# Order and cut of the first loads in a decode step: a 512 KB block of keys first, wq in four transfers, head 0's values in two

## The chip, the core and the metric

The kernel runs on one core of one Trainium2 chip. The core has five engines with a program each: TensorE (PE in the profile, its weight loads PEld), VectorE (DVE), ScalarE (ACT), GpSimd (POOL) and SyncE (SP), which here does little but issue transfers. Transfers between HBM and the on-chip memory SBUF run on 16 DMA engines that all issuers share. SBUF has 128 partitions; a transfer moves one row, a run of bytes, into each. The metric is the device time of one execution in microseconds (us); lower is better.

## What is computed

One token goes through an attention block with a key and value cache and through a gated feed-forward block:

```
h  = x + Attention(layernorm(x), k_cache, v_cache, wq, wo)
     q = layernorm(x) @ wq                      # 512 -> 32 heads of 128
     scores = q . k * 128**-0.5                 # 8 key heads, 65536 positions, 4 query heads for each
     o = softmax(scores) . v
     Attention = o @ wo                         # 4096 -> 512
h2 = h + (sigmoid(hn @ w_gate) * (hn @ w_up)) @ w_down,  hn = layernorm(h)
```

All inputs are bf16. The caches are 8 heads of 65,536 positions of 128 values, 16.78 MB for one head's keys and as much for its values; wq and wo are 4.19 MB each, the three feed-forward matrices 1.84 MB each. Together 282.33 MB are read once, for one token.

## The kernel before

**Staging.** A *chunk* is 2,048 positions of one head: 512 KB, on each partition 16 positions or 4 KB. A head's keys are 32 chunks, its values too. They pass through `ring`, a buffer of 36 chunks; `ktw` holds first wq (4 MB), then, as 8 chunk slots, the transposed keys, and last wo. A head is loaded in halves of 16 chunks (8.39 MB): K.0, V.0 of the head before, K.1, V.1 of the head before. Head 0's keys differ: they come in four transfers of 8 chunks into free space of the ring and wait for nothing.

**Loading.** All large loads are issued by SyncE, one after the other, in the order in which they are written (lines 341 to 374). A load that overwrites space waits for its last reader: an `F` mark of VectorE (line 528, a tiny memset to `scr` that stands behind the last transpose of a region) or a `PV` mark of TensorE. SyncE stops at such a wait, and all issues behind it stop too. Head 1's first keys wait for F0.0, which stands behind 16 transposes of head 0; head 0's first values wait for F0.1, behind 32. The first load of SyncE (wq) and the first of ScalarE (x) are moved ahead of the barrier at the program's start.

**Which position lies where.** In a transfer partition p takes a contiguous run of the cache, so a transfer of 16 chunks gives partition p the positions 256p to 256p+255 of its half. Softmax does not care for the order of positions as long as keys and values of one head use the same.

**Compute of a head.** VectorE transposes each chunk in 32x32 blocks from `ring` to `ktw` (line 525), TensorE multiplies it with the query weights (line 443, four passes for each chunk, in groups of four chunks), VectorE takes the maximum, ScalarE the exponentials (line 571), VectorE transposes them, and TensorE multiplies them with the values (line 443 again, `ring` and `PT_sb`). ScalarE copies a head's query weights into `ktw` (`head_weights`, line 494) behind the exponentials of the head before. Chunks are taken in the order 4 to 15, 0 to 3, 16 to 31.

**Start.** x is loaded into `xs` and spread by a small matmul (line 423) and two VectorE operations to `x_col`, where partition p holds the elements 4p to 4p+3. Layernorm makes `xz` of it (line 432). TensorE then projects q (`project_q`, line 466): 32 matmuls over wq, whose partition p holds the rows 4p to 4p+3. q goes through ScalarE and a VectorE transpose (lines 480, 483) into `qz`, and only then is `ktw` free for the first transposed keys: head 0's first transpose waits for q.

Of the kernel before, what the change touches and what calls it, by code (L numbers as in the profile page):

```python
# [9 lines left out]
AF = mybir.ActivationFunctionType  # L10
ALU = mybir.AluOpType
# [4 lines left out]
NQ = 32  # L16
DH = 128
# [3 lines left out]
TC = 16  # L21
# [3 lines left out]
NKT = 8  # L25
# [10 lines left out]
class Prog:  # L36
# [14 lines left out]
    def op(self, eng, fn, deps=(), name=None, to=None, times=1):  # L51
        assert name is None or name not in self.where, name
        self.ops[eng].append(dict(fn=fn, deps=[d for d in deps if d], name=name, dma=None, to=to, times=times, part=self.part.get(eng)))
        if name:
            self.where[name] = (eng, len(self.ops[eng]) - 1)

    def dma(self, eng, fn, sem, deps=(), name=None):
        self.op(eng, fn, deps, name)
        rec = self.dma_sems.setdefault(sem, dict(sem=None, count=0))
        rec["count"] += 16  # L60
        self.ops[eng][-1]["dma"] = (sem, rec["count"])
# [162 lines left out]
def bass_sequential_preLN__gqa_block_cached__glu_gated_glu__decode_kernel(  # L224
# [10 lines left out]
    CH = TC * DH  # L235
    PIECES = ((0, 16), (16, 32))
# [10 lines left out]
    with ExitStack() as es:  # L247
# [3 lines left out]
        gsel = sb("gsel", [128, 128], fp32)  # L251
        hz = sb("hz", [128, 128], fp32)
        identf = sb("identf", [128, 128], fp32)
        onesf = sb("onesf", [128, 128], fp32)
        lsel = sb("lsel", [128, 128], fp32)
        iota_i = sb("iota_i", [128, 128], i32)
        ident = sb("ident", [128, 128], bf16)
# [6 lines left out]
        ring = sb("ring", [128, RING], bf16)  # L264
        ktw = sb("ktw", [128, NKT * CH + WH], bf16)
# [3 lines left out]
        qz = sb("qz", [128, 8 * 64], bf16)  # L269
# [2 lines left out]
        one_f = sb("one_f", [1, 1], fp32)  # L272
        zcol = sb("zcol", [128, 1], bf16)
        zf = sb("zf", [128, 1], fp32)
        XR = 16
        xs = sb("xs", [XR, D // XR], bf16)
        xpick = sb("xpick", [XR, 128], bf16)
        xmask = sb("xmask", [128, 128 // XR], fp32)
        xm = sb("xm", [128, D // XR], fp32)
        x_col = sb("x_col", [128, 4], fp32)  # L280
        xz = sb("xz", [128, 4 * 16], bf16)
        qh = sb("qh", [32, 512], bf16)
        qt = sb("qt", [32, 512], bf16)
        hT = [sb(f"hT{i}", [128, 4], fp32) for i in range(2)]
        sq = sb("sq", [128, 4], fp32)
        st = [sb(f"st{i}", [128, 2], fp32) for i in range(2)]
        mo = [sb(f"mo{i}", [128, 4], fp32) for i in range(2)]
        rstd = [sb(f"rstd{i}", [128, 1], fp32) for i in range(2)]
# [26 lines left out]
        def ps(bank, c0, c1, p0=0, p1=128):  # L315
            return PS[p0:p1, bank * 512 + c0: bank * 512 + c1]
# [5 lines left out]
        op, dma = P.op, P.dma  # L322


        dma("act", lambda e: e.dma_start(xs[:, :], A_x[0].rearrange("o (s j) -> (o s) j", s=XR)), "x", name="x")
        W_SPLIT = {"wg": [(0, 4)], "wu": [(0, 4)]}
# [6 lines left out]
        def load(k, h, q, deps, sem, name, cols=None):  # L333
            j0, j1 = PIECES[q]
            a, z = cols or (j0, j1)
            cache = A_k_cache if k == "K" else A_v_cache
            rows = cache[0, h, j0 * TC * 128:j1 * TC * 128, :].rearrange("(p t) d -> p (t d)", p=128)
            at = (first_chunk(k, h, q) - j0) * CH
            dma("sp", lambda e: e.dma_start(ring[:, at + a * CH:at + z * CH], rows[:, (a - j0) * CH:(z - j0) * CH]), sem, deps, name)

        dma("sp", lambda e: e.dma_start(ktw[:, 0:NKT * CH].rearrange("p (k n) -> p k n", k=4),
                                        A_wq.rearrange("(p k) n -> p k n", p=128)), "r0", (), "wq")
        for q in range(2):
            for i in range(2):
                j0 = 16 * q + 8 * i
                load("K", 0, q, (), f"r{2 * q + i + 1}", f"K0.{q}{'ab'[i]}", (j0, j0 + 8))
        for h in range(1, HKV):
            load("K", h, 0, ["F0.0" if h == 1 else f"F{h - 1}.1"], "ka", f"K{h}.0")
            load("V", h - 1, 0, ["F0.1" if h == 1 else f"PV{h - 2}.3"], "va", f"V{h - 1}.0")
            load("K", h, 1, [f"F{h}.0"], "kb", f"K{h}.1")  # L350
            load("V", h - 1, 1, [f"PV{h - 1}.1"], "vb", f"V{h - 1}.1")
        h = HKV - 1
# [11 lines left out]
        for k, w in (("wg", B_w_gate), ("wu", B_w_up)):  # L364
            src = w.rearrange("(p k) n -> p (k n)", p=128)
            for i, (k0, k1) in enumerate(W_SPLIT[k]):
                at = W_AT[k]
                dma("sp", lambda e, at=at, w=src, a=k0 * FF, z=k1 * FF: e.dma_start(ring[:, at + a:at + z], w[:, a:z]),  # L368
                    f"{k}{i}", [f"PV{HKV - 1}.1"] if k == "wg" else (), f"{k}.{i}")
        src = B_w_down.rearrange("(p r) n -> p r n", p=128)  # L370
        for i, (r0, r1) in enumerate(WD_SPLIT):
            at = AT["wd"] * CH
# [33 lines left out]
        def ln_rstd(i, bank, c0, factor):  # L406

            op("dve", lambda e: e.tensor_scalar(mo[i][:, 0:2], ps(bank, c0, c0 + 2), 1.0 / D, None, op0=ALU.mult),
               [f"tot.{i}"], f"mo.{i}")
            op("dve", lambda e: e.tensor_tensor(mo[i][:, 2:3], mo[i][:, 0:1], mo[i][:, 0:1], ALU.mult), [f"mo.{i}"], f"m2.{i}")  # L410
            op("dve", lambda e: e.tensor_tensor(mo[i][:, 3:4], mo[i][:, 1:2], mo[i][:, 2:3], ALU.subtract), [f"m2.{i}"], f"var.{i}")
            op("dve", lambda e: e.tensor_scalar(ve[i][:, :], mo[i][:, 3:4], eps, factor, op0=ALU.add, op1=ALU.mult),  # L412
               [f"var.{i}"], f"ve.{i}")
            op("pool", lambda e: e.tensor_tensor(rstd[i][:, :], ve[i][:, :], nhalf[:, :], ALU.pow), [f"ve.{i}", "nhalf"],  # L414
               f"rstd.{i}")


        n = 128 // XR
        op("dve", lambda e: e.tensor_copy(xpick[:, :].rearrange("s (u i) -> s u i", i=n),
# [8 lines left out]
        op("dve", lambda e: None, ["zf"])  # L428
        ln_stats(0, (x_col[:, :], bass.AP(tensor=zf, offset=0, ap=[[1, 128], [0, 4]])), "xcol", 0, 0)
        ln_rstd(0, 0, 0, 1.0)  # L430
        xz_dst = bass.AP(tensor=xz, offset=31, ap=[[4 * 16, 128], [-8, 4]])
        op("dve", lambda e: e.tensor_scalar(xz_dst, hT[0][:, :], mo[0][:, 0:1], rstd[0][:, 0:1], op0=ALU.subtract,
                                            op1=ALU.mult), ["rstd.0", "xz0"], "xz")
        def addr_of(t, elements=0):
            return nc.lookup_mloc(t).addr + 2 * elements

# [39 lines left out]

        op("act", lambda e: e.activation(ps(1, 0, 512, 0, 8), bass.AP(tensor=zcol, offset=0, ap=[[1, 8], [0, 512]]), AF.Copy), ["zcol"], "zq")
        op("act", lambda e: e.activation(ps(5, 0, 512), bass.AP(tensor=zcol, offset=0, ap=[[1, 128], [0, 512]]), AF.Copy), (), "zy")
        op("pe", project_q, ["zq", "zy", "xz", "wq", "identf", "lsel", "onef", "sel", "gsel", "row", "PTz", "qz0"], "q")
        op("act", lambda e: e.activation(  # L480
            bass.AP(tensor=qh, offset=0, ap=[[512, 8], [64, 8], [32, 2], [1, 32]]), psap(1, 0, [[64, 8], [1, 2], [2, 32]], 0, 8), AF.Copy),
           ["q", "qh0"], "qh")
# [7 lines left out]
        def head_weights(h):  # L490

            dst = bass.AP(tensor=ktw, offset=W0 + NC - 1, ap=[[KTW_ROW, 128], [WJ, 4], [NC, 16]])
            src = bass.AP(tensor=qz, offset=64 * h, ap=[[512, 128], [16, 4], [1, 16]])
            op("act", lambda e: e.activation(dst, src, AF.Copy), ["qz", "Wz"] if h == 0 else (), f"W{h}", to="W")

        def clear_out(h):

# [10 lines left out]
        def dve_block(b):  # L508
            h, r = b // NR, b % NR
            for c in range(NC):  # L510
                n, s = b * NC + c, r * NC + c
                j = ORDER[s]
                q = sum(j >= z for _, z in PIECES)
                at = (first_chunk("K", h, q) + j - PIECES[q][0]) * CH
                src = ring[:, at:at + CH].bitcast(fp32)
                dst = ktw[:, (n % NKT) * CH:(n % NKT + 1) * CH].bitcast(fp32)
                if h == 0:
                    deps = [f"K0.{q}{'ab'[j % 16 // 8]}"] if s in (0, 4, 16, 24) else []
                    if s == 0:
                        deps.append("q")  # L520
                else:
                    deps = [f"K{h}.{q}"] if s in (0, 16) else []
                if r:
                    deps.append(f"S{b - 1}.{c}")
                op("dve", lambda e, d=dst, sr=src: e.transpose(d, sr), deps, f"T{b}.{c}", to="T")  # L525
                mark = ({15: 0, 31: 1} if h == 0 else {11: 0, 27: 1}).get(s)
                if mark is not None:
                    op("dve", lambda e, m=4 * h + mark: e.memset(scr[:, m:m + 1], 0.0), (), f"F{h}.{mark}")  # L528
            if b % NR == NR - 1:
                for k in range(NR):  # L530
                    u = b - NR + 1 + k
                    op("dve", lambda e, u=u: e.tensor_reduce(M_sb[:, u % 4:u % 4 + 1], ps(u % NS, 0, 512), AX.X, ALU.max),  # L532
                       [f"S{b}.{NC - NR + k}"], f"mx{u}", to="D")
                op("dve", lambda e: e.memset(scr[:, 32 + b // NR:33 + b // NR], 0.0), (), f"G{b // NR}")
# [255 lines left out]
        for i in range(HKV + 1):  # L790
            loop, last = 0 < i < HKV, i == HKV
            for r in range(NR):
# [26 lines left out]
                if not last and r == 3:  # L819
# [9 lines left out]
                                                   op0=ALU.mult, op1=ALU.add), ["tot.1"], "hc")  # L829
# [6 lines left out]
        for i, (nm, bank) in enumerate((("wg", GB), ("wu", UB))):  # L836
            at = W_AT[nm]
            for kt in range(4):
                for c in range(4):
# [3 lines left out]
                        rhs=ring[:, at + kt * FF + c * FG: at + kt * FF + (c + 1) * FG],  # L843
                        start=(kt == 0), stop=(kt == 3), tile_position=(0, 32 * c)),
# [66 lines left out]
```

## Time and profile before

| | |
|---|---|
| median of 3 runs (lowest, highest) | 656.7 us (656.45, 657.0) |
| the profiled execution, its own time | 656.39 us |
| span of the profile | 655.1 us |
| TensorE busy (matmuls) | 403.4 us, 62% |
| VectorE busy | 350.4 us, 53% |
| ScalarE busy | 43.1 us, 7% |
| mean granted clock of TensorE | 0.779 |

The span runs from the first to the last instruction of the profiled execution; the rest of its own time lies before and after. Busy shares are means over the whole span and do not say which engine sets the end: VectorE and TensorE work on a head's chunks side by side, and each waits for the other and for transfers in turn. The page also gives the packets and bytes of each DMA queue, and a chain of waits that is followed back from the last instruction to whatever released it, step by step. A transfer in that chain is counted from its issue to its landing, also while it only stands behind others.

### The profile page before, as it was taken

The page shows a single profiled execution, that of the slowest core. Times are in us where ns is not written, and L with a number is a line of the kernel's source. Part 1 is how long each engine was busy: PE and PEld are TensorE (multiplying, and loading weights), DVE is VectorE, ACT ScalarE, POOL GpSimd, SP SyncE. Part 2 cuts the span into 40 slices and gives each one's busy share as a digit, 9 for nine tenths or more (in the row PEclk, how much of TensorE's full clock was granted, in tenths as well). Part 3 has the DMA queues.
Part 4 walks back from the last instruction along what each step waited for, and adds up shares of the span by engine and source line. Part 5 has one row for each costly group of instructions (what it writes and reads, how often), then busy time and mean ns, then how long its engine had stood idle before and what let it go on. Part 6 is the DMA issues. An engine that isn't in the chain of part 4 may idle for free.

```text
span 655.1 us, 6215 instructions
## 1 busy us (share of the span) xinstructions
PE 403.4 (62%) x2317; PEld 65.8 (10%) x1549; DVE 350.4 (53%) x428; ACT 43.1 (7%) x114; POOL 3.7 (1%) x19
## 2 busy tenths in 40 slices
PE   2698672938648293774828467392855839285466
PEld 0100010110101000010100101010010101001122
DVE  3399853819366290935719184481917548093202
ACT  1100200020000200002000200002000020001001
POOL 1000000000000000000000000000000000000000
PEclk9899795966959588685968769596885959779665
DMA  9999999998999999999999999999999999999998
GB/s 386 446 422 474 420 412 448 448 448 388 444 448 448 436 396 448 448 448 400 432 448 448 436 396 448 448 448 408 424 448 448 444 392 444 448 448 424 422 407 363
DMA packets 6372, 282.33 MB, mean 431 GB/s; under 512 B 738, under 2 KB 868, under 8 KB 1252
## 3 DMA queue, kind: packets, MB, share of 16 engines
q1 hardware_dynamic: 6340, 282.33, 99.7%
q10 hardware_dynamic: 32, 0.00, 0.0%
HBM read 282.33 MB, written 0.00 MB: 431 GB/s over the span
## 4 chain that ended last, share of the span: by engine, by line
DMA 63%; DVE 32%; PE 3%; issue 1%; SPq 0%; ACT 0%; PEldq 0%
DMA ring<-in_A_k_cache_dram 53%; DVE ktw L525 32%; DMA ring<-in_B_w_down_dram 5%; DMA ring<-in_A_v_cache_dram 4%; PE PS L443 3%; DMA ktw<-in_A_wq_dram 2%; SPq L373 0%; SPq L368 0%; ACT qh L480 0%; PE PS L860 0%; PE PS L475 0%; DVE y_sb L878 0%; PEldq L171 0%; DVE scr L528 0%; DVE qt L483 0%
## 5 line engine op out<-in xcount | busy, mean ns | idle before, releaser
L525 DVE STREAM_TRANSPOSE ktw<-ring 128x1024 f32<-128x1024 f32 x256 | 291.6, 1207 | 160.3 <-DMA ring<-in_A_k_cache_dram 160.2
L443 PE MATMUL PS<-ktw 128*128 128x512 bf16 x1024 | 276.7, 421 | 156.6 <-DVE ktw L525 156.5
L443 PE MATMUL PS<-ring,PT_sb 128*32 x1024 | 87.7, 432 | 55.4 <-issue 46.5
L443 PEld LDWEIGHTS PS<-ktw 128*128 x256 | 26.3, 103 | 395.8 <-issue 233.5
L612 ACT ACTIVATE po_sb<-PS,rl 128x512 bf16<-128x512 f32 x8 | 5.5, 687 | 523.6 <-PE PS L443 523.6
L443 PEld LDWEIGHTS PS<-ring,PT_sb 128*32 x1024 | 20.6, 116 | 119.5 <-issue 118.2
L560 DVE TENSOR_REDUCE gmj<-PS 1x4 f32<-1x128 f32 x8 | 2.2, 279 | 54.3 <-PE PS L558 54.3
L532 DVE TENSOR_REDUCE M_sb<-PS 128x1 f32<-128x512 f32 x32 | 19.9, 683 | 19.3 <-PE PS L443 19.3
L571 ACT ACTIVATE P_sb<-PS,negmax 128x512 bf16<-128x512 f32 x32 | 21.6, 686 | 0.3
L581 DVE STREAM_TRANSPOSE PT_sb<-P_sb 128x512 bf16<-128x512 bf16 x32 | 19.9, 677 | 1.5 <-ACT P_sb L571 1.5
L443 PE MATMUL PS<-ktw,xz 128*8 x32 | 12.7, 459 | 6.5 <-DMA ktw<-in_A_wq_dram 5.9
L483 DVE STREAM_TRANSPOSE qt<-qh 32x512 bf16<-32x512 bf16 x1 | 0.7, 700 | 18.4 <-ACT qh L480 18.4
L628 DVE TENSOR_TENSOR Lw<-O,blk_of 128x896 bf16<-128x896 bf16 (+1 forms) x2 | 1.4, 683 | 16.0 <-ACT O L618 16.0
L637 DVE CAST O<-PS 128x28 bf16<-128x28 f32 (+1 forms) x2 | 0.4, 176 | 13.2 <-PE PS L634 13.2
L558 PE MATMUL PS<-identf,gm 128*1 128x128 f32 x16 | 4.3, 364 | 4.9 <-issue 2.8
L565 PE MATMUL PS<-one_f,gmrep 1*128 1x1 f32 x16 | 4.2, 331 | 5.0 <-DVE gmrep L562 5.0
L571 ACT ACTIVATION_READ_ACCUMULATOR P_sb<-PS,negmax 128x1 f32 x32 | 6.5, 202 | 0.0
L615 PE MATMUL PS<-sel_bf,po_sb 128*128 128x4 bf16 x32 | 2.1, 171 | 6.3 <-ACT po_sb L612 6.3
L498 ACT ACTIVATE PS<-zcol 128x512 f32<-128x512 bf16 x8 | 5.0, 621 | 0.0
L586 PE MATMUL PS<-L_sb,lsel 128*128 128x4 f32 x16 | 2.5, 229 | 3.8 <-DVE PT_sb L581 3.8
L414 POOL TENSOR_TENSOR rstd<-ve,nhalf 128x1 f32<-128x1 f32 x2 | 1.1, 557 | 643.8 <-DVE ve L412 643.8
L588 DVE TENSOR_REDUCE lsum<-PS 128x1 f32<-128x4 f32 x8 | 1.3, 162 | 6.4 <-PE PS L586 6.4
(90 smaller groups left out, 67.4 us busy)
## 6 DMA issues: line engine op xcount, KB each, us to landing
ring<-in_A_k_cache_dram SPq DMA_DIRECT2D x4, 4096.0 KB, 34.8
ring<-in_A_v_cache_dram SPq DMA_DIRECT2D x1, 5120.0 KB, 30.1
ktw<-in_A_wq_dram SPq DMA_DIRECT2D x1, 4096.0 KB, 12.3
ktw<-in_A_wo_dram SPq DMA_DIRECT2D x1, 3584.0 KB, 18.4
ring<-in_A_v_cache_dram SPq DMA_DIRECT2D x1, 3072.0 KB, 36.9
ring<-in_B_w_gate_dram SPq DMA_DIRECT2D x1, 1792.0 KB, 23.8
ring<-in_B_w_up_dram SPq DMA_DIRECT2D x1, 1792.0 KB, 27.6
ring<-in_B_w_down_dram SPq DMA_DIRECT2D x1, 1024.0 KB, 29.6
```

Of the source, the lines that this page charges most:

```text
L443: return e.add_instruction(mybir.InstMatmult(name=nc.get_next_instruction_name(), engine=mybir.EngineType.PE, ins=[rhs, lhsT], outs=[e.low ...
L498: op("act", lambda e: e.activation(ps(PO, 0, 512), bass.AP(tensor=zcol, offset=0, ap=[[1, 128], [0, 512]]), AF.Copy), ["zcol"] if h == 0 e ...
L525: op("dve", lambda e, d=dst, sr=src: e.transpose(d, sr), deps, f"T{b}.{c}", to="T")
L532: op("dve", lambda e, u=u: e.tensor_reduce(M_sb[:, u % 4:u % 4 + 1], ps(u % NS, 0, 512), AX.X, ALU.max), [f"S{b}.{NC - NR + k}"], f"mx{u}" ...
L558: op("pe", lambda e: e.matmul(ps(MISC, 0, 128, 0, 1), lhsT=gm[:, :], rhs=identf[:, :], start=True, stop=True), [f"gm{h}"], f"gmT{h}", to="Q")
L560: op("dve", lambda e: e.tensor_reduce(gmj[:, :], ps(MISC, 0, 128, 0, 1).rearrange("p (i a c) -> p a i c", a=4, c=NC), AX.XY, ALU.max), [f" ...
L565: op("pe", lambda e: e.matmul(ps(MISC, 128, 129), lhsT=gmrep[0:1, :], rhs=one_f[0:1, 0:1], start=True, stop=True), [f"gmrep{h}"], f"neg{h}")
L571: op("act", lambda e, b=b: e.activation(P_sb[:, (b % 4) * 512:(b % 4 + 1) * 512], ps(b % NS, 0, 512), AF.Exp, bias=negmax[:, k:k + 1], sca ...
L581: op("dve", lambda e, b=b: e.transpose(PT_sb[:, (b % 4) * 512:(b % 4 + 1) * 512], P_sb[:, (b % 4) * 512:(b % 4 + 1) * 512]), [f"E{b}"], f" ...
L586: op("pe", lambda e: e.matmul(ps(MISC, 132, 136), lhsT=lsel[:, :], rhs=L_sb[:, :], start=True, stop=True), [f"PT{NR * h + NR - 1}"], f"l{h ...
L612: op("act", lambda e: e.activation(po_sb[:, :], ps(PO, 0, 512), AF.Copy, scale=rl[:, :]), [f"PV{h}.{NR - 1}", f"rl{h}"], f"po{h}", to="po")
L615: op("pe", lambda e, t=t: e.matmul(ps(OX, 0, 4), lhsT=po_sb[:, t * 128:(t + 1) * 128], rhs=sel_bf[:, 8 * t:8 * t + 8:2], start=(t == 0), s ...
```

## The change

- The first transfer of SyncE is now the contiguous first chunk of head 0's keys (positions 0 to 2,047, 16 on each partition, "K0.0c"). The other 15 chunks of that half are taken from the positions behind it, 7 in K0.0a and 8 in K0.0b, so their rows are 28 KB and 32 KB.
- wq follows in four transfers, each of 128 rows of the matrix, one row of 8 KB on each partition. Partition p now holds the rows p, 128+p, 256+p and 384+p, and x must lie in the same way for the projection: `xs` becomes [4, 128], and one more matmul with an identity ("xq") turns it into four columns, from which `xz` is made. The statistics of layernorm still come from `x_col`, over wider intermediate tiles.
- Head 0's values must lie as its keys do: chunk 0 comes as a transfer of its own ("V0.0c") behind the wait for F0.1, the other 15 chunks in a second one.
- Head 0's transpose of chunk 0 also waits for K0.0c, and head 1's copy of the query weights on ScalarE for V0.0c.

```
-        XR = 16
+        XR = 4
...
+            c0 = j0
+            if h == q == 0:
+                first = TC * 128
+                c0, keys = (0, (0, first)) if z == 1 else (1, (first, PIECES[0][1] * TC * 128))
+                rows = cache[0, h, keys[0]:keys[1], :].rearrange("(p t) d -> p (t d)", p=128)
+            dma("sp", lambda e: e.dma_start(ring[:, at + a * CH:at + z * CH], rows[:, (a - c0) * CH:(z - c0) * CH]), sem, deps, name)
...
-        dma("sp", lambda e: e.dma_start(ktw[:, 0:NKT * CH].rearrange("p (k n) -> p k n", k=4),
-                                        A_wq.rearrange("(p k) n -> p k n", p=128)), "r0", (), "wq")
+        load("K", 0, 0, (), "r5", "K0.0c", (0, 1))
+        for k in range(4):
+            dma("sp", lambda e, k=k: e.dma_start(ktw[:, k * NQ * DH:(k + 1) * NQ * DH], A_wq[128 * k:128 * k + 128, :]), "r0", (), f"wq{k}")
...
-                load("K", 0, q, (), f"r{2 * q + i + 1}", f"K0.{q}{'ab'[i]}", (j0, j0 + 8))
+                load("K", 0, q, (), f"r{2 * q + i + 1}", f"K0.{q}{'ab'[i]}", (max(j0, 1), j0 + 8))
...
-            load("V", h - 1, 0, ["F0.1" if h == 1 else f"PV{h - 2}.3"], "va", f"V{h - 1}.0")
+            if h == 1:
+                load("V", 0, 0, ["F0.1"], "vc", "V0.0c", (0, 1))
+            load("V", h - 1, 0, ["F0.1" if h == 1 else f"PV{h - 2}.3"], "va", f"V{h - 1}.0", (1, 16) if h == 1 else None)
...
+        op("pe", lambda e: e.matmul(ps(7, 48, 52), lhsT=xs[:, :], rhs=ident[0:XR, 0:XR], start=True, stop=True), ["x", "ident"], "xq")
...
-        op("dve", lambda e: e.tensor_scalar(xz_dst, hT[0][:, :], mo[0][:, 0:1], rstd[0][:, 0:1], op0=ALU.subtract,
-                                            op1=ALU.mult), ["rstd.0", "xz0"], "xz")
+        op("dve", lambda e: e.tensor_scalar(xz_dst, ps(7, 48, 52), mo[0][:, 0:1], rstd[0][:, 0:1], op0=ALU.subtract,
+                                            op1=ALU.mult), ["rstd.0", "xz0", "xq"], "xz")
...
-        op("pe", project_q, ["zq", "zy", "xz", "wq", "identf", "lsel", "onef", "sel", "gsel", "row", "PTz", "qz0"], "q")
+        op("pe", project_q, ["zq", "zy", "xz", "wq3", "identf", "lsel", "onef", "sel", "gsel", "row", "PTz", "qz0"], "q")
...
-            op("act", lambda e: e.activation(dst, src, AF.Copy), ["qz", "Wz"] if h == 0 else (), f"W{h}", to="W")
+            op("act", lambda e: e.activation(dst, src, AF.Copy), ["qz", "Wz"] if h == 0 else ["V0.0c"] if h == 1 else (), f"W{h}", to="W")
...
+                    if j == 0:
+                        deps.append("K0.0c")
```

SyncE's issues at the program's start, where the order of all transfers is set, before (line, destination and source, partitions x elements, and what the issue waits for; `s_dve` are VectorE's marks):

```order
L341 DMA ktw<-in_A_wq_dram 128x16384
L215 UNCONDITIONAL_BRANCH [waits barrier_Pool_Activation_PE_DVE_SP_release]
L339 DMA ring<-in_A_k_cache_dram 128x16384 x4
L339 DMA ring<-in_A_k_cache_dram 128x32768 [waits s_dve]
L339 DMA ring<-in_A_v_cache_dram 128x32768 [waits s_dve]
```

and the same place with the change, where the lines are numbered anew:

```order
L344 DMA ring<-in_A_k_cache_dram 128x2048
L215 UNCONDITIONAL_BRANCH [waits barrier_Pool_Activation_PE_DVE_SP_release]
L348 DMA ktw<-in_A_wq_dram 128x4096 x4
L344 DMA ring<-in_A_k_cache_dram 128x14336
L344 DMA ring<-in_A_k_cache_dram 128x16384 x3
L344 DMA ring<-in_A_k_cache_dram 128x32768 [waits s_dve]
L344 DMA ring<-in_A_v_cache_dram 128x2048 [waits s_dve]
L344 DMA ring<-in_A_v_cache_dram 128x30720
```

Only the chunk of keys is now ahead of the barrier, wq has moved behind it, and five more transfers stand in the queue.

ScalarE at the end of head 0 and the start of head 1, before (L571 the exponentials, L494 head 1's weight copy, L612 head 0's output):

```order
L567 ACTIVATE negmax<-PS 128x1 [waits s_pe]
L571 ACTIVATE P_sb,L_sb<-PS,negmax 128x512 [waits s_act]
L571 ACTIVATE P_sb,L_sb<-PS,negmax 128x512 x3
L494 ACTIVATE ktw<-qz 128x4x16
L612 ACTIVATE po_sb<-PS,rl 128x512 [waits s_dve,s_pe]
```

and with the change:

```order
L578 ACTIVATE negmax<-PS 128x1 [waits s_pe]
L582 ACTIVATE P_sb,L_sb<-PS,negmax 128x512 [waits s_act]
L582 ACTIVATE P_sb,L_sb<-PS,negmax 128x512 x3
L503 ACTIVATE ktw<-qz 128x4x16 [waits d_vc]
L623 ACTIVATE po_sb<-PS,rl 128x512 [waits s_dve,s_pe]
```

The instructions stand where they stood; the copy has a wait for a transfer (`d_vc`, the value chunk) that it did not have.

More of the change, by code (lines that the diff above doesn't have):

```diff
@@ L338, in load @@
             at = (first_chunk(k, h, q) - j0) * CH
-            dma("sp", lambda e: e.dma_start(ring[:, at + a * CH:at + z * CH], rows[:, (a - j0) * CH:(z - j0) * CH]), sem, deps, name)
-        dma("sp", lambda e: e.dma_start(ktw[:, 0:NKT * CH].rearrange("p (k n) -> p k n", k=4),
-                                        A_wq.rearrange("(p k) n -> p k n", p=128)), "r0", (), "wq")
+            c0 = j0
[7 more added lines that the diff above has]
+            dma("sp", lambda e, k=k: e.dma_start(ktw[:, k * NQ * DH:(k + 1) * NQ * DH], A_wq[128 * k:128 * k + 128, :]), "r0", (), f"wq{k}")
         for q in range(2):
```

## The prediction

> **What bounds the kernel now.** I read the queue totals first, then the chain of waits, then the windows.
>
> The page's queue totals:
>
> ```profile
> span 655.1 us, 6215 instructions
> q1 hardware_dynamic: 6340, 282.33, 99.7%
> HBM read 282.33 MB, written 0.00 MB: 431 GB/s over the span
> ```
>
> One queue, the one SyncE feeds, carries all the bytes, and its packets fill 99.7% of the time of 16 DMA engines. The sum of packet times is therefore the candidate for the bound. The chain of waits, in order of time, seems to say something else, since it gives VectorE a third of the span:
>
> ```profile
> 0.00 12.30 DMA ktw<-in_A_wq_dram
> 12.30 0.57 issue
> ...
> 27.80 16.03 DVE ktw L525 x15
> 43.83 0.87 issue
> ...
> 45.94 24.47 DMA ring<-in_A_k_cache_dram
> 70.41 0.02 issue
> 70.44 13.20 DVE ktw L525 x12
> ...
> 84.14 24.85 DMA ring<-in_A_k_cache_dram
> 109.00 0.02 issue
> ...
> 586.36 24.97 DMA ring<-in_A_v_cache_dram
> 611.33 0.03 issue
> ...
> 622.70 30.29 DMA ring<-in_B_w_down_dram
> 652.99 0.04 issue
> 653.04 0.52 PE PS L860 x10
> ```
>
> The landings decide: head 1's key halves land at 70.41 and 109.00, 38.6 us apart, with one 8.39 MB value transfer and one 8.39 MB key transfer between, that is 16.78 MB at 435 GB/s. A transfer of 8.39 MB thus takes 19.3 us, while the chain charges 24.47 us to it: the first 5 us it only stood behind others. VectorE's share is time in which the queue was busy with something else. Whole stages, by window (columns: length, busy us of PE, PEld, DVE, ACT, POOL, granted clock, DMA share, GB/s):
>
> ```profile
> 0.00:1.00 1.00, 0.00 (x0) 0.00 (x0) 0.00 (x0) 0.00 (x0) 0.20 (x4) 1.00 0.00 0
> 1.00:2.00 1.00, 0.00 (x0) 0.00 (x0) 0.67 (x3) 0.95 (x1) 0.98 (x10) 1.00 1.94 524
> 1.02:11.49 10.47, 0.79 (x3) 0.60 (x3) 5.04 (x22) 2.39 (x3) 2.92 (x14) 1.00 0.98 398
> 11.49:21.17 9.68, 8.07 (x20) 1.66 (x20) 0.00 (x0) 0.00 (x0) 0.00 (x0) 1.00 1.00 430
> 21.17:30.85 9.68, 5.50 (x16) 1.18 (x14) 3.68 (x4) 3.22 (x7) 0.00 (x0) 0.84 1.00 433
> 100.00:600.00 500.00, 304.63 (x1724) 45.28 (x1100) 274.88 (x311) 28.09 (x78) 0.00 (x0) 0.77 1.00 434
> ```
>
> The share is 1.00 from 11.5 us on. So the end is set by when the first byte flows (1.0 us), by the sum of all transfers, and by some 2 us of work after the last landing at 652.99. Nothing on TensorE, VectorE or ScalarE moves the end unless SyncE issues a transfer so late that the queue runs dry. The sums below start from this execution's own time, 656.39 us (span 655.1 and 1.3 around it); the median of the runs is 656.7, 0.3 above, and I add changes to the median.
>
> **The change, part by part.** *Bytes:* none added or removed. *Cut of the transfers:* wq goes from rows of 32 KB per partition to four transfers with rows of 8 KB; head 0's chunk 0 of keys and of values, 0.52 MB each, get rows of 4 KB, and the rest of those transfers rows of 28 and 60 KB. Rows of these lengths are found in the tail, where wo's last 4 KB rows and w_down's first 8 KB rows are moved:
>
> ```profile
> 640.20:643.90 3.70, 2.87 (x28) 0.51 (x20) 0.00 (x0) 0.69 (x2) 0.00 (x0) 0.50 1.00 430
> 648.40:650.40 2.00, 1.62 (x20) 0.38 (x16) 0.45 (x1) 0.64 (x1) 0.00 (x0) 0.50 1.01 426
> 638.90:639.50 0.60, 0.00 (x0) 0.00 (x0) 0.00 (x0) 0.00 (x0) 0.00 (x0) 0.50 1.01 416
> 651.00:651.40 0.40, 0.32 (x2) 0.03 (x1) 0.37 (x2) 0.00 (x0) 0.00 (x0) 0.50 1.00 407
> ```
>
> 14 KB rows run at 430, 8 KB at 426, 4 KB at 416, 3 KB at 407 GB/s; 32 KB rows at 433 above. wq: 4.19 MB / 426 = 9.85 us against 9.69 at 433, +0.16. Each 0.52 MB chunk: 1.26 us at 416 against 1.21, +0.05, twice. The 28 KB and 60 KB rows lie between 430 and 434: +0.04 for both together. Sum **+0.3 us**. Bounds: 0 if the small differences are rounding of windows, +0.5 if I read 8 KB at 420 (+0.30) and 4 KB at the 3 KB rate (+0.08 each). I take +0.3, as the rates fall in order with the row.
>
> *Five more transfers* (47 issues for 42 on this queue, counting by the order of SyncE). What does a boundary between queued transfers cost? From 611.33 to 652.99, 41.66 us, ten transfers follow each other (4.19 MB of wo in two, 8.39 MB of values in two, 5.51 MB of gate, up and down in six): 18.09 MB, 434 GB/s, the rate of the long ones. Short ones are among them, by the page's list of issues (KB each, us to landing):
>
> ```profile
> ktw<-in_A_wo_dram SPq DMA_DIRECT2D x1, 512.0 KB, 37.7
> ring<-in_B_w_down_dram SPq DMA_DIRECT2D x1, 256.0 KB, 30.3
> ```
>
>  So a boundary costs nothing while a later transfer is queued; I take 0. At most it costs what the first transfer lost to its start: 10.47 us against 9.68 for the next of the same size, 0.79 us each.
>
> A page of the Trainium skill, "DMA: Bandwidth & Descriptors" (Anatomy of one DMA), speaks against this edit: it fits each DMA as some 2.0 us fixed plus its bytes at 436 GB/s, half efficiency near 860 KB. By it five more transfers would be up to 10 us more, an estimate from that page. The ten in the tail, four of them of 0.52 MB or less, do not show it: the fixed part hides behind the queue.
>
> *Is anything queued in time at the start?* SyncE's row of issues:
>
> ```profile
> 0.00 0.40 SPq L341 DMA_DIRECT2D ktw<-in_A_wq_dram  x1
> 0.92 2.56 SPq L339 DMA_DIRECT2D ring<-in_A_k_cache_dram  x4
> ```
>
> The first issue at 0.00 gives bytes from 1.0 us; the next comes only at 0.92, behind the barrier, and four take 2.56 us, 0.64 each. Today 4 MB cover that gap, afterwards 0.5 MB. The second transfer, by the first one's delay, can flow from 1.9 us; the chunk keeps the engines busy for 1.26 us after 1.0 and the 0.79 of start, to 3.0 us. Each wq quarter then covers 2.46 us against 0.64 per issue. No gap, by 1.1 us.
>
> *Head 0 starts later.* TensorE's projection waits for the last quarter of wq. That lands 1.26 + 0.16 = 1.4 us later, 13.7 instead of 12.30, and with it q, the 32 transposes of head 0 and its softmax. The x path grows (128x128 instead of 128x32, one matmul more):
>
> ```profile
> 5.38 0.19 DVE L424 TENSOR_TENSOR xm<-PS,xmask 128x32 f32<-128x32 f32 x1 [0.59 <-PE PS L423]
> 8.43 0.29 DVE L432 TENSOR_SCALAR xz<-hT,mo,rstd 128x4 bf16<-128x4 f32 x1 [0.68 <-POOL rstd L414]
> 64.01 0.33 SPq L339 DMA_DIRECT2D ring<-in_A_v_cache_dram  x1
> 73.38 0.49 ACT L494 ACTIVATE ktw<-qz 128x64 bf16<-128x64 bf16 x1
> ```
>
> xz is done at 8.72 and some tenths later afterwards, 5 us ahead of wq: free. Without that cover its growth, under 0.5 us, would be a delay of q and again no delay of the end, for what counts is the issue behind head 0. Head 1's first keys are issued at 45.94 when 16 transposes are done; they land at 70.41 and need 19.3 us, so their bytes began at 51.1. Less 1.0 us from issue to first byte, the slack is 4.2 us; start and landing of the first transfer together leave 1.6 us unexplained (12.30 - 1.0 - 9.69), and if all of it is landing, 2.6 us. The shift of 1.4, less the 0.2 by which the queue itself is longer, stays below. Head 0's first values (64.01) have a slack of 3.8 to 5.4 the same way (their turn comes at 68.8 to 70.4), and the second key half (84.14 against 89.7) 3.0 to 4.6. All of it is **0 us** on the end.
>
> *The added wait.* Head 1's weight copy on ScalarE now waits for the value chunk; behind it stand head 0's output and later exponentials, and TensorE's first scores of head 1 wait for the copy. The copy ran at 73.38 and will be ready at 74.8 for head 0's delay. The chunk flows right behind head 1's keys: 70.41 + 0.2 + 1.3 = 71.9. The wait is over 2.9 us before it is reached: 0.
>
> Total: 656.4 + 0.3 = 656.7 for a profiled execution, **657.0 us** beside the median.
>
> **The rivals.**
>
> *A shorter start.* The first transfer lost 0.79 us to its neighbour and nothing flowed for 1.0 us. If short rows or a contiguous block start the engines sooner, up to 0.79 comes back: 657.0 - 0.8 = 656.2. For it: only this transfer is below 430. Against: the lag may be the same for any first transfer. Recovering part of the first 1.0 us too would give 655.2; the first issue stands where it stood, so this is unlikely.
>
> *Every transfer pays a start.* 5 x 0.79 = 4.0 us: 661.0. For it only the first transfer; against it the ten of the tail. The skill's fixed part per DMA named above would be this case.
>
> *The queue runs dry before head 1* (the one that ends on the other side by a new wait). Place: the issue at 45.94. It decides from a shift of q or of head 0's transposes beyond 2.8 us, 1.4 of which are spent, and costs 1 us per us beyond. Head 0's pace hangs on TensorE's clock, 0.84 in the window from 21 us; half a clock for 10 us more would slow 16 transposes by some 4 us, a shift of 5.4, and 2.6 us dry: 659.6. For it: the chain already has VectorE standing 0.87 us at 43.83, one transpose short of the issue. Against: nothing in the change asks more of TensorE than one small matmul.
>
> **How the numbers follow.** Forecast 0.68 (its own range 656.6 to 657.5); shorter start by up to 0.8, 0.10; by more, 0.07; each transfer pays 0.06; queue dry 0.09. A difference under 0.2%, 1.3 us, is about what a measurement of this kernel can tell from no change: the forecast and the 0.8 us gain lie within, so same 0.78, faster 0.07, slower 0.15. The range 656.0 to 658.2 holds the forecast, the short start and the mild end of a dry queue, about 0.8.
>
> **What would show it.** Right: DMA share 1.00 from some 12 us on, landings 38.6 us apart as now, the first of them at 70.6 to 70.8, last landing near 653.3, projection from some 14 us. Wrong: a window below 400 GB/s near 3 us (no cover), near 50 us (queue dry) or at each wq quarter (a boundary costs); a first window above 398 GB/s with an earlier last landing (shorter start).

## The result and the profile after

The changed kernel takes 659.03 us (median of 7 runs, 658.3 to 660.16) against 656.53 us before (7 runs, 656.23 to 657.0): ratio 1.0038, 95% interval 1.0028 to 1.0048. It is slower by 2.5 us. The forecast was 657.0 us in a range to 658.2, "no difference" as the likeliest case. The profiled execution took 660.16 us with a span of 657.9; 2.26 us of it lie outside the span, where the other six runs have 1.28 to 1.36, so the spans are what to compare: 657.0 to 657.9 in seven runs, 655.1 in the profile before.

The chain of waits of the changed kernel in order of time (start, length, what), the places that the prediction read before:

```profile
2.42 13.37 DMA ktw<-in_A_wq_dram
15.79 0.57 issue
16.36 6.11 PE PS L452 x15
...
87.78 24.08 DMA ring<-in_A_k_cache_dram
111.87 0.02 issue
...
625.92 29.89 DMA ring<-in_B_w_down_dram
655.82 0.04 issue
```

wq lands at 15.79 instead of 12.30, where 13.7 was forecast. Head 1's second key half lands at 111.87 instead of 109.00, 2.87 us late, and the last transfer at 655.82 instead of 652.99, 2.83 late. From the one to the other it is 543.95 us after and 543.99 before: **everything was lost before 112 us**, and the other 540 us are the same.

The windows of the changed kernel (columns as in the prediction):

```profile
1.00:3.00 2.00, 0.00 (x0) 0.00 (x0) 1.47 (x5) 1.76 (x2) 1.81 (x12) 1.00 0.95 308
3.00:5.50 2.50, 0.26 (x1) 0.10 (x1) 2.24 (x10) 0.63 (x2) 0.55 (x3) 1.00 0.68 262
5.50:7.00 1.50, 0.60 (x3) 0.59 (x3) 0.66 (x5) 0.00 (x0) 0.00 (x0) 1.00 1.00 350
7.00:13.00 6.00, 0.10 (x1) 0.01 (x1) 0.92 (x5) 0.00 (x0) 0.56 (x1) 1.00 1.01 426
```

and of the kernel before at the same place:

```profile
3.00:5.50 2.50, 0.20 (x1) 0.10 (x1) 1.85 (x9) 0.45 (x1) 0.39 (x1) 1.00 0.98 420
```

Between 3 and 5.5 us the DMA engines are busy for 0.68 of the time and move 262 GB/s instead of 420. The single packets in the trace say how: twelve engines go from the chunk's 4 KB rows to wq's 8 KB rows between 2.7 and 3.3 us; four have no packet from some 2.7 to 5.5 us. A queue with work in it, and four of its sixteen engines without any. SyncE's issues in the same trace:

```profile
0.00 0.40 SPq L344 DMA_DIRECT2D ring<-in_A_k_cache_dram  x1
1.10 1.76 SPq L348 DMA_DIRECT2D ktw<-in_A_wq_dram  x4
...
49.07 0.33 SPq L344 DMA_DIRECT2D ring<-in_A_k_cache_dram  x1
```

The second issue comes at 1.10 us (0.92 before), and its first packet 1.6 us later. Head 1's first keys are issued at 49.07 instead of 45.94, 3.1 us late where 1.4 was forecast: late enough for a second place to be suspected, a queue that runs dry near 51 us.

### The profile page after: what moved, and what is told of

It is laid out like the page before. It is cut to its first block, busy times and chain, and to the rows that moved or that the text cites. A ratio compares the mean times of both kernels' runs of the same rounds, so it can differ in the third digit from the quotient of the medians.

```text
span 657.9 us, 6224 instructions
## 1 busy us (share of the span) xinstructions
PE 402.6 (61%) x2318; PEld 65.4 (10%) x1550; DVE 350.6 (53%) x428; ACT 43.1 (7%) x114; POOL 3.7 (1%) x19
## 4 chain that ended last, share of the span: by engine, by line
DMA 59%; DVE 32%; PE 6%; issue 2%; ACT 1%; SPq 0%; PEldq 0%
DMA ring<-in_A_k_cache_dram 49%; DVE ktw L536 31%; PE PS L452 5%; DMA ring<-in_B_w_down_dram 5%; DMA ring<-in_A_v_cache_dram 4%; DMA ktw<-in_A_wq_dram 2%; ACT P_sb L582 0%; DVE M_sb L543 0%; SPq L348 0%; SPq L381 0%; SPq L376 0%; PE PS L576 0%; ACT qh L489 0%; PE PS L871 0%; PE PS L569 0%
## 5 line engine op out<-in xcount | busy, mean ns | idle before, releaser
L571 DVE TENSOR_REDUCE gmj<-PS 1x4 f32<-1x128 f32 x8 | 2.2, 279 | 53.5 <-PE PS L569 53.5
```

What stands on the lines that cost most here:

```text
L571: op("dve", lambda e: e.tensor_reduce(gmj[:, :], ps(MISC, 0, 128, 0, 1).rearrange("p (i a c) -> p a i c", a=4, c=NC), AX.XY, ALU.max), [f" ...
```

## The experiments

All were timed beside the kernel before on the same chip (656.54 to 656.63 us in the three groups of four). Two theories stood at the beginning: A, that the four idle engines are those on which x, now in four rows, falls; B, that the chunk is over before the next transfer's descriptors (the orders that a DMA engine works off) reach all engines, and that an engine which ran dry resumes late.

**x in 16 rows again.** `xs` as before, and four matmuls that put it in place:

```
+        for a in range(4):
+            op("pe", lambda e, a=a: e.matmul(ps(7, 48, 52, 32 * a, 32 * a + 32), lhsT=xs[:, :], rhs=ident[0:XR, a:XR:4], ..., tile_position=(0, 32 * a)), ...)
```

> The changed kernel, but x comes in 16 rows as before (spread over all DMA engines) and four small matmuls put it in place. In the trace of the change four of the 16 engines stand idle from about 2.7 to 5.5 us. Theory A (x, cut into four rows, falls on four engines and holds those back): all 16 engines move from 3 us on, wq lands near 13.7 instead of 15.8, the projection starts near 14 instead of 16.4, head 1's keys are issued near 47.2 instead of 49.1, time 656.7 to 657.3. Theory B (the 512 KB chunk is over before wq's descriptors reach all engines, and an engine that ran dry restarts late): no change, DMA share 0.75 from 3 to 5.5 us, time 658.3 to 659.5.

Measured 660.08 us (ratio 1.0055, 1.0038 to 1.0072). wq lands at 15.86, head 1's second keys at 112.85. A falls, but the time lies above both theories' ranges, and the loss looks otherwise here: the share is 0.98 from 3 to 5.5 us, at 347 GB/s; a few engines start up to 1.8 us late, and some packets of 8 KB take 1.4 us where 0.31 is usual. Why this kernel loses 3.4 us and not 2.5 is open.

**x in 4 rows alone, in the kernel before.**

> The kernel before, with nothing changed but x in four rows of 256 B instead of 16 of 64 B. Theory A: four engines lose some 2.7 us at the start, time 658 to 659.5. Theory B: wq's 4 MB in front cover everything, time as before, 656.3 to 656.9.

656.80 us (1.0002, 0.9993 to 1.0012). Behind wq's 4 MB, x in four rows costs nothing; with the run above, it is not the cause. It does move the second issue: 1.10 us here, 0.93 in the run above with 16 rows, 0.92 before. ScalarE's issue of x, ahead of the barrier, takes 0.56 us with four rows and 0.38 with 16. The 0.17 us do not decide, since the loss was no smaller at 0.93.

**The first quarter of wq ahead of the chunk.** One swap of two transfers:

```
-        load("K", 0, 0, (), "r5", "K0.0c", (0, 1))
         for k in range(4):
             dma(... wq{k} ...)
+            if k == 0:
+                load("K", 0, 0, (), "r5", "K0.0c", (0, 1))
```

> The changed kernel, with the first quarter of wq (1 MB) as the first transfer and the 512 KB chunk of keys second. Theory B (too short a first transfer): 1 MB covers the gap to the second issue, no engine stands idle, time 656.7 to 657.3. Theory A (x on four engines): the same four engines are late again behind the first transfer, time 658.3 to 659.5.

656.77 us (1.0008, 0.9998 to 1.0017; one of its ten runs took 659.32). The window and the landing of head 1's second keys in its trace:

```profile
3.00:5.50 2.50, 0.26 (x1) 0.10 (x1) 2.25 (x10) 0.63 (x2) 0.56 (x3) 1.00 0.99 406
```

```profile
85.51 23.53 DMA ring<-in_A_k_cache_dram
109.04 0.02 issue
```

The engines are all busy, the landing is back at 109.04 (109.00 before). Everything else of the change is in this kernel: five more transfers, short rows, the x path, the cut values, the added wait on ScalarE. Together they cost 0.2% at most. B stands, as far as it speaks of a gap and of late engines; descriptors are not seen in a trace.

**wq in one transfer** of 512 rows of 8 KB, behind the chunk:

> The changed kernel, with wq as a single transfer of 512 rows of 8 KB in the same places, still behind the chunk. Theory C (four issues close on each other, or the number of transfers, is what leaves engines without work): DMA share 1.00 from 3 us on, time 656.7 to 657.3. Theories A and B: four engines still idle until about 5.5 us or longer, since a transfer of 4 MB has four times the descriptors to make, time 658.3 or more.

659.43 us (1.0043, 1.0026 to 1.006), with a share of 0.53 from 3 to 5.5 us:

```profile
3.00:5.50 2.50, 0.26 (x1) 0.10 (x1) 2.24 (x10) 0.63 (x2) 0.56 (x3) 1.00 0.53 180
```

Nine engines are without packets here, until 4.7 to 5.3 us. The number of wq's transfers is not the cause; theory C falls.

**Two issues ahead of the barrier.** Order and sizes of the change, but wq's first quarter is issued at 0.45 us instead of 1.10:

```
-        first = self.ops["sp"].pop(0)
-        put("sp", nc.sync, first, [])
+        for _ in range(2):
+            first = self.ops["sp"].pop(0)
+            put("sp", nc.sync, first, [])
...
+        code[at[0]:at[0]] = loads
```

> The changed kernel, with the same order of transfers, but the first quarter of wq is issued ahead of the barrier too, right behind the chunk, some 0.6 us earlier than at 1.10 us. Theory B (the gap between the first and the second issue, not order or size): no engine idle between 3 and 5.5 us, wq lands near 13.5, time 656.6 to 657.3. If size or order of the first transfer matters by itself: 658.3 to 659.5 as the changed kernel.

656.49 us (0.9999, 0.999 to 1.0009). SyncE's issues and the window:

```profile
0.00 0.40 SPq L345 DMA_DIRECT2D ring<-in_A_k_cache_dram  x1
0.45 2.32 SPq L349 DMA_DIRECT2D ktw<-in_A_wq_dram  x4
```

```profile
3.00:5.50 2.50, 0.26 (x1) 0.10 (x1) 2.28 (x9) 0.81 (x2) 0.73 (x3) 1.00 1.01 406
```

The same 512 KB first, 0.65 us less to the second issue, and the whole loss is gone. It is the gap to the second issue, not what is loaded or in which order.

**Two chunks first**, 1 MB in rows of 8 KB (`first = 2 * TC * 128`, and the other cuts to match):

> The changed kernel, with two chunks of keys (1 MB, rows of 8 KB) as the first transfer, and head 0's values cut to match. Theory B: 1 MB lasts until the second transfer's descriptors are there, no engine idle at the start. wq lands near 14.8 and head 1's keys are issued near 48.5, short of the queue's end near 50.5, so time 656.8 to 657.8. If a transfer of keys ahead of wq is itself the cause: 659 or more.

658.42 us (1.0027, 1.0015 to 1.0038), more than B alone allows. The start is whole (416 GB/s from 3 to 5.5 us), but head 0 still starts late (wq lands at 14.63, where 12.30 was before), and the loss has moved to head 1:

```profile
3.00:5.50 2.50, 0.26 (x1) 0.10 (x1) 2.24 (x10) 0.63 (x2) 0.56 (x3) 1.00 1.00 416
```

```profile
47.91 0.33 SPq L344 DMA_DIRECT2D ring<-in_A_k_cache_dram  x1
```

```profile
85.61 24.59 DMA ring<-in_A_k_cache_dram
110.21 0.02 issue
```

By the packets, only 8 to 13 of the sixteen engines work between 50.5 and 51.2 us; the last one takes up head 1's keys at 51.51 us, 3.6 us after their issue (50.75 in the kernel before).

**Two chunks first, 24 of 32 projection matmuls** (`e.Fori(0, 3 * HKV)`; the last quarter of wq is left out of q):

> Two chunks of keys first (no engine idle at the start, 658.42 us), with 24 of the 32 projection matmuls (the last eight left out). Head 0 starts 3.2 us sooner and head 1's keys are issued near 45 us. Theory D (with two chunks first, what was left is the queue that runs dry near 50 us): the rate from 50 to 54 us is back at 430 or more, time 656.6 to 657.2. If two chunks cost by themselves: 658 or more.

656.58 us (1.0001, 0.9991 to 1.001). Head 1's keys are issued at 45.47, and the second half lands where it did before the change:

```profile
84.28 24.86 DMA ring<-in_A_k_cache_dram
109.14 0.02 issue
```

From 50 to 56 us, first here, then with all 32 matmuls (a packet counts whole where it starts, and those of 64 KB take 2.4 us, so these rates only compare with each other):

```profile
50.00:56.00 6.00, 5.23 (x23) 0.58 (x6) 6.00 (x6) 0.00 (x0) 0.00 (x0) 1.00 1.21 524
50.00:56.00 6.00, 5.24 (x24) 0.48 (x5) 6.00 (x7) 0.00 (x0) 0.00 (x0) 1.00 1.06 415
```

So what two chunks cost is the late issue behind head 0: a queue that runs dry near 50.5 us, 1.8 us.

**The changed kernel with 24 of 32 projection matmuls** (the same edit, q lacks the same part):

> The changed kernel, with 24 of the 32 projection matmuls (the last eight are left out, so q lacks that part of its sum). Head 0 starts 3.2 us sooner, head 1's keys are issued near 45.9 as before the change, and only the loss at the start is left. Theory B alone: 658.3 to 659.3 as the changed kernel. Theory D: the part that the dry queue costs is gone, 657.3 to 658.3.

658.68 us (1.0033, 1.002 to 1.0045). Head 1's keys are issued at 46.60, as in the kernels that lose nothing there, and 2.1 us stay, in B's range and not in D's. In its trace all sixteen engines work from 48 to 54 us, so the start alone makes them. Against 659.03 for the whole change, 0.35 us are left for the dry queue, less than the intervals can tell apart.

**The projection late, otherwise the kernel before**: eight matmuls more, written out one by one.

> The kernel before, with eight matmuls more behind the projection of q (into an accumulator that is not read), so that head 0 starts some 3.2 us later while all transfers stand as they stood. Head 1's keys are then issued near 49.1 us, as in the changed kernel, instead of 45.94. Theory D (besides the idle engines of the start, the changed kernel pays for a queue that runs dry near 51 us): the rate from 51 to 56 us falls below 400 GB/s, time 657.3 to 659. Theory B alone (the start is all): time as before, 656.3 to 656.9.

660.78 us (1.0062, 1.0045 to 1.0079), but this time cannot be used: the spans of the four runs are 655.5 to 655.7 us, and 4.9 to 5.3 us lie outside the span instead of 1.3. Head 1's keys were issued near 47.7, not at 49.1, and its second half landed at 109.51. Its spans are some 0.3 us above those of the kernel before beside it (655.3 in the middle), so a delay of 1.7 us cost little there. The question was asked again with a loop in place of written-out matmuls.

**Two issues ahead of the barrier, the projection late** by a loop of eight matmuls:

```
+            with e.Fori(0, 8):
+                e.matmul(ps(6, 0, 512, 0, 8), lhsT=qz[:, 0:8], rhs=qz[:, 0:512], start=True, stop=True, skip_group_check=True)
```

> Two issues ahead of the barrier (656.49 us, no engine idle at the start), with a loop of eight more matmuls behind the projection (into an accumulator that is not read), so that head 0 starts some 3 us later and head 1's keys are issued near 49.5 us. Theory D: the queue runs dry near 51 us, span 1 to 2.5 us longer than the 655.1 of two issues ahead alone. If a dry queue costs only when the start was lost too: span 655 to 655.6.

658.44 us (1.0029, 1.0017 to 1.004), spans 656.7 to 657.3, with 1.3 to 1.6 us outside. All engines work at the start, and the issue behind head 0 is late:

```profile
49.84 0.33 SPq L345 DMA_DIRECT2D ring<-in_A_k_cache_dram  x1
```

```profile
87.84 22.93 DMA ring<-in_A_k_cache_dram
110.77 0.02 issue
```

3.1 us later than in the same kernel without the loop (46.75), a landing 1.8 us later (108.99 there), 1.95 us more in the median. No engine has a packet from 50.5 to 50.8 us. A dry queue before head 1 costs by itself, as D says.

**What makes an engine late: the issues that follow?** The second quarter of wq held back to 3.5 us:

> The changed kernel, with the second quarter of wq issued only near 3.5 us (it waits for a VectorE operation of the start), so that nothing follows the first quarter's issue for 2 us. Theory E (engines without work wait because the following issues crowd the making of descriptors): the late engines start the first quarter near 3 us instead of 5.5, time 657 to 658.3. Theory F (an engine that has run dry takes that long by itself): late engines at 5 us or more as before, time 658.3 to 659.5.

658.69 us (1.003, 1.0019 to 1.0042). Neither theory has it right: the time is in F's range, but with nothing issued behind the first quarter, nine idle engines resume at 4.0 to 4.7 us, sooner than 5.5 but still some 3 us after the issue at 1.10, and the second quarter then comes too late for some once more (291 GB/s from 5.5 to 7.5 us). Nor does it show that the following issues matter. The kernel with 24 projection matmuls has the changed kernel's program for its first microseconds, with nothing held back, and in its trace twelve engines stood idle behind the chunk and resumed at 3.2 to 4.1 us. How many engines are late, and for how long, differs between executions of the same start.

**And when all engines are idle?** The first quarter itself held back:

> The changed kernel, with the first quarter of wq issued only near 3.5 us, when every engine has finished the chunk. Theory F1 (an engine without work starts as at the program's start, 1.0 to 1.8 us after the issue): all 16 start between 4.5 and 5.4 us, no engine is later than the others, time 658.3 to 659.3. Theory F2 (an engine that ran dry takes some 3 to 4 us from the issue): first packets of wq at 6.5 us or later, 660 or more.

658.77 us (1.0035, 1.0022 to 1.0048). F1 holds:

```profile
3.63 2.00 SPq L348 DMA_DIRECT2D ktw<-in_A_wq_dram  x4
```

```profile
3.00:4.50 1.50, 0.00 (x0) 0.00 (x0) 1.44 (x7) 0.63 (x2) 0.56 (x3) 1.00 0.00 0
4.50:5.50 1.00, 0.26 (x1) 0.10 (x1) 0.80 (x5) 0.00 (x0) 0.00 (x0) 1.00 0.77 131
```

Nothing moves from 2.9 to 4.6 us; then all sixteen engines start, between 4.6 and 5.3, 1.0 to 1.7 us after the issue. Here every engine lost some 2.2 us, and head 1's second keys landed at 111.42, 2.42 late. In the changed kernel the sixteen engines lost 0.7 us in the mean but the four late ones some 2.8, and the landing was 2.87 late: the end waits for the slowest engine, not for the mean. What an engine loses it does not make up. Each moves 8 of the 128 rows of such a transfer, and in the trace of the changed kernel the first engine takes up head 1's keys at 50.81 us and the last at 52.99, where it was 50.21 and 50.75 before.

## Why the prediction was wrong

The step that failed is the paragraph "Is anything queued in time at the start?". It let the second transfer flow 1.0 us after its issue at 0.92, found the chunk lasting to 3.0, and concluded: "No gap, by 1.1 us". Three numbers in it were wrong. The issue stood at 1.10. Its first packet came 1.6 us after it, at 2.7, just when the first engines had finished the chunk. And the engines that were not reached by then did not start within some tenths, but at 5.5 (at 3.2 to 4.1 in the other trace of this start). I had taken the first transfer's start on an idle machine for the start of a transfer behind another, and an average over 16 engines for each of them. The measured price is 2.1 us, by the kernel with the shorter projection.

The same step left the price of being wrong out: a gap at the start stands among the signs ("no cover"), but no rival has it, with a time or a chance. It is paid by a few engines only, but these set the end, and the wq landing that waits for them pushes head 0 back as well.

**The queue before head 1** was a rival at 0.09. The mechanism is real and was sized too kindly: I let it decide from a shift beyond 2.8 us and cost 1 us per us. With two chunks first a shift of 2.0 us (47.91 against 45.94) already cost 1.8 us, and issues at 46.6 to 46.8 cost nothing, so the threshold lies between 0.9 and 2.0. I had reckoned 1.0 us from issue to first byte there too, and the keys' turn at 51.1. Their turn came at 50.2 to 50.8 in the kernel before, and from the issue to the last engine's first packet it took 3.6 us with two chunks first and 2.0 with two issues ahead and the late projection, where the queue was empty.

**The two losses do not add up.** The start alone costs 2.1 us; a dry queue alone, by the issue at 49.84, 1.95; the change has both, its issue at 49.07, and loses 2.5. While the queue is dry, the engines that were late at the start still have rows of the keys to move, so they lose little there. That this is the reason is read from the packets of one trace, not from a run of its own.

**What held.** Five more transfers cost nothing behind a full queue (the list of DMA issues has 44 loads before and 49 after, not 42 and 47; the difference is right). Without the gap wq landed at 13.34 and 13.52, near the 13.7 forecast. The +0.3 us for short rows is not seen: with wq's first quarter ahead, head 1's second keys, behind all the transfers that were cut anew, land 0.04 us later than before, and with two issues ahead of the barrier 0.01 sooner (108.99). That the last landing is 653.38 against 652.99 in the first of these comes from behind 109 us, where nothing was changed. The x path was free for q: `xz` was finished at 8.73 us (8.72 before). The added wait was over before it was reached: the copy on ScalarE ran at 76.72, directly behind the last exponential. The stages from head 1 on are unchanged to a few hundredths.

The fixed part for each DMA in the Trainium skill's "DMA: Bandwidth & Descriptors" (Anatomy of one DMA), some 2.0 us, was set aside in the prediction because ten transfers in the tail do not show it. That is right for a queue with work in it. That section of the Trainium skill fits the figure for transfers that GpSimd issues and puts most of it at a transfer's end, in the confirmation of the last bytes, which the prediction does not say. What cost time here is a delay at the other end: 1.0 to 1.7 us from issue to first packet when all engines stood idle, more on engines that had run dry. The rule for bandwidth on the same page of the Trainium skill (Rules for kernel authors) is 1 MiB or more for a DMA; here 1 MB as the first transfer covered the gap and 512 KB did not, though 512 KB did as soon as the next issue followed at 0.45 us.

No version beat both kernels. The best of the changed forms, two issues ahead of the barrier, is at 0.9999 of the kernel before, within an interval of 0.1% to each side: the first chunk ahead of wq brings nothing even where it costs nothing.

## What to carry to other kernels

This DMA-bound kernel lost its time where engines had nothing to move, so look at the first microseconds and at every issue that waits for compute, and take for each the latest of the 16 engines, not their mean. A first transfer must last until the second one can start on every engine: put a large one first, or issue the second right behind it. Work that is delayed at the start delays every issue that hangs on it: reckon its shift against the slack of the next dependent transfer, with a wide margin for the time from issue to first byte.

## What the runs showed of the hardware

- Four to twelve of the sixteen engines that had run out of rows while others still worked resumed 2 to 4.4 us after the issue of their next transfer (3.2 to 5.5 us, in four traces), but 1.0 to 1.7 us after it when all were idle. Why they resume later then is open.
- Eight matmuls written out behind the projection added some 3.8 us outside of the span (655.6 us, 0.3 more than before); a loop of eight did not (1.3 to 1.6 us outside, as usual). Why is not known.
- Near 50 us it is the same: with two chunks first, some engines ran out of rows 2.4 us after the issue of the next transfer, and the last of them resumed 3.6 us after it. So an issue 2.0 us later than before the change cost 1.8 us although 0.9 us of such a delay cost nothing.
